# A re-ordered instruction plan and more filler matmuls at the start of a window-attention and gated-FFN kernel

## The chip, the cores and the metric

The kernel runs on one core of one Trainium2 chip. The metric is the device time of one execution, in microseconds (us). The engines are TensorE (PE in the profile, its weight loads PEld), VectorE (DVE), ScalarE (ACT), GpSimd (POOL) and SyncE (SP), whose queue issues every DMA of this kernel.

## The reference

Attention over a causal window of 64 tokens, eight batches of 576 tokens with eight heads of 64, and then a gated feed-forward layer on the 4608 resulting rows:

```python
scores = scale * np.matmul(q, k.transpose(0, 1, 3, 2))
mask = (rel >= 0) & (rel < window)                      # window = 64
scores = np.where(mask, scores, -1000000000.0)
attn = softmax(scores); x = np.matmul(attn, v)          # x: 4608 x 512
h = x @ w_in                                            # 512 x 2048, float64 values
sp = np.maximum(h, 0.0) + np.log1p(np.exp(-np.abs(h)))  # softplus
out = (h * erf(sp)) @ w_out                             # 2048 x 512, float64 values
```

## The kernel before

Every product is made from a high and a low float16 part (three matmuls for one), with power-of-two scales that come from the largest magnitudes of the data. Attention works in 36 units u of 128 tokens. Two units are a chunk c of 256 tokens, and each chunk goes through the feed-forward layer in two halves of the hidden width, so there are 36 groups g.

The weights arrive as float64 and are turned into scaled float16 pairs on the chip, in 16 pieces u of 1 MB (pieces 0 to 7 of `w_in`, 8 to 15 of `w_out`). This conversion runs beside the first units of attention, and the stretch up to about 200 us in which it goes on is called the prologue here.

Nothing is scheduled at run time. `PLAN` is one string of tokens; each token calls one handler, and each engine executes its instructions in the order in which the tokens stand. A number after the name is the unit, piece, group or pair, and a last letter is the engine (a ScalarE, v VectorE, g GpSimd). The tokens that matter below:

- `L` loads a weight piece; `lq lk lv` load q, k and v of a unit; `t` and `xt` are transposing transfers of the attention weights and of x. All of them are on SP's queue.
- Weight conversion: `g` makes a plane of sign bits (one buffer, so one piece at a time), `d` builds the low bits from it, and `dd` does both on VectorE without the plane; `c` rebiases, `o` assembles, `b` takes the largest magnitude. For each pair of pieces `mb` (TensorE), `mx` (VectorE), `my` (TensorE) and `mc` (VectorE) turn that into a scale on all partitions. `dg` (a scaled diagonal) and `h` make the high part, `lp` (TensorE) and `le`, or `l`, the low part.
- Chunk scale: `pk` peaks of q, k and v, then `pa` (VectorE), `pb` (TensorE), `px` (VectorE), `py` (TensorE), `pc` (VectorE).
- Attention: `qh ql kh kl vh vl` the float16 parts, `s` scores, `m` masked maximum, `f e r` softmax, `a` weights times v, `n` normalize, `xh xl` the parts of x.
- Feed-forward: `mm:g:p` the first matmuls (24 for each p of 0 to 3), `ev` their eviction, `sp er gt gh gl` the gate, `mA mB` the second matmuls, `fo st` the result.
- `wm:k:n` is n matmuls of the identity into an unused part of a PSUM tile, which nothing reads. They only keep TensorE occupied.

The PSUM tile `av` holds five things: the output of `a`, the small rows and columns written by `pb`, `py`, `mb` and `my`, and the target of `wm`:

```python
    crow, call = avb[:3, 0, row_at:row_at + P], avb[:, 0, row_at + P:row_at + P + 3]
    wrow, wall = avb[:1, 1, row_at:row_at + P], avb[:, 1, row_at + P:row_at + P + 1]
    idle = avb[:, 0, row_at + P + 3:row_at + P + 123]
    ...
    def warm(k, n):
        for _ in range(n):
            nc.tensor.matmul(idle, ident, ident[:, :120], start=True, stop=True)
```

An instruction that reads `av` waits for TensorE by a count. In the built program this count reaches to the last TensorE instruction that wrote `av` ahead of the reader in `PLAN`, and matmuls of `wm` are among those: where a `wm` token stands between `py` and `pc`, `pc` waits for the end of that `wm`.

Of the kernel before, what the change touches and what calls it, by code (L numbers as in the profile page):

```python
# [19 lines left out]
W = 64  # L20
# [193 lines left out]
def window_attention_gated_ffn(ctx, tc, q, k, v, w_in, w_out, masks, out):  # L214
# [195 lines left out]
    def expo(u, par):  # L410
        s, es = smi(u, par), cde[u // TPC][:, 1:2]
        nc.scalar.activation(pp[0][u % 2][:, HP * par:HP * par + HP, :], s, AF.Exp, bias=shift14, scale=es)  # L412
        nc.scalar.activation(s, s, AF.Exp, bias=shift14, scale=es)  # L413
# [298 lines left out]
```

## Time and profile before

| | us |
|---|---|
| median of 3 runs | 932.47 (932.11 to 933.4) |
| the profiled execution, its own time | 931.69 |
| its span, first to last instruction | 929.5 |
| TensorE busy | 897.9 (97%), of which 32.7 are `wm` (line 643, 507 matmuls) |
| VectorE, ScalarE, GpSimd busy | 714.7, 634.4, 290.8 |
| mean granted TensorE clock | 0.993 |

Time outside the span is 2.2 us (931.69 less 929.5). A row of a timeline gives the start and the length of instructions in us, then engine, line, operation, and output <- input by tile; in brackets is how long the engine was idle just before, and who released it. The line numbers of `wm` are 643 before and 647 after the change, those of the other functions behind `expo` move by four as well.

### The profile page before, as it was taken

To read this page: it belongs to the slowest core of one execution; us is meant where nothing else is said; L and a number is where in the kernel's file an instruction comes from. 1 tells how busy PE (TensorE), PEld (TensorE's weight loads), DVE (VectorE), ACT (ScalarE), POOL (GpSimd) and SP (SyncE) were. 2 spreads that over 40 slices of the span, in tenths; PEclk is the share of its full clock that TensorE was granted. 3 is DMA by queue.
4 is the path that set the end of the run, shared out by engine and by line. 5 is a ranking of instruction groups with operands and counts; after the bars stand their busy time and mean duration, and the time that the engine had idled before them with its cause. 6 is when DMAs were issued, how large, how long until landed. Compare 5 with 4: busy or idle time off the path is not lost.

```text
span 929.5 us, 22240 instructions
## 1 busy us (share of the span) xinstructions
PE 897.9 (97%) x9281; PEld 603.5 (65%) x9281; DVE 714.7 (77%) x1506; ACT 634.4 (68%) x749; POOL 290.8 (31%) x299
## 2 busy tenths in 40 slices
PE   8779998999999999999999999999999999999998
PEld 8546566656766666667666767566667566766663
DVE  6989887988888998785976876986876976845443
ACT  4888976888675886959764758764768764924333
POOL 1343333425244353441330541330541430501000
PEclk9989999999999999999999999999999999999999
DMA  9585747144443555445353525352625250301000
GB/s 366 171 199 182 202 86 197 41 96 132 112 129 81 114 128 124 84 111 102 93 86 102 113 88 103 92 92 102 112 84 103 91 105 33 70 23 24 24 23 23
DMA packets 140532, 98.63 MB, mean 106 GB/s; under 512 B 117776, under 2 KB 117904, under 8 KB 140432
## 3 DMA queue, kind: packets, MB, share of 16 engines
q1 hardware_dynamic: 140432, 97.22, 42.2%
q8 instruction: 72, 1.18, 0.5%
q14 instruction: 28, 0.23, 0.1%
HBM read 59.44 MB, written 9.44 MB: 74 GB/s over the span
## 4 chain that ended last, share of the span: by engine, by line
PE 79%; DVE 10%; DMA 5%; ACT 3%; issue 1%; POOL 1%; DVEq 0%; POOLq 0%; ACTq 0%
PE hp L590 36%; PE o L626 35%; PE av L427 3%; PE s L394 2%; DMA vr<-v_in 2%; PE o L553 1%; DMA stage<-w_out 1%; DVE y L610 1%; DMA qr<-q_in 1%; DVE gl L322 1%; DMA xt<-xs 1%; DMA stage<-w_in 1%; DVE vs L322 1%; DVE sm L403 1%; DVE stage L504 1%
## 5 line engine op out<-in xcount | busy, mean ns | idle before, releaser
L590 PE MATMUL hp<-xt,w 128*128 128x256 f16 x3456 | 401.8, 274 | 7.8 <-DMA xt<-xs 3.6
L590 PEld LDWEIGHTS <-w 128*128 128x128 f16 x3456 | 336.7, 98 | 70.4 <-issue 11.4
L626 PE MATMUL o<-w,gh 128*128 128x512 f16 x1152 | 260.9, 379 | 2.5 <-DVE w L444 1.8
L626 PEld LDWEIGHTS <-gh 128*128 128x128 f16 x1152 | 110.3, 98 | 125.8 <-issue 2.4
L317 DVE TENSOR_SCALAR h<-hp,c 128x512 f32<-128x512 f32 x123 | 90.9, 745 | 79.4 <-PE hp L590 79.0
L626 PE MATMUL o<-w,gl 128*128 128x512 f16 x576 | 136.4, 380 | 0.0
L602 ACT ACTIVATE y<-h 128x1024 f32<-128x1024 f32 x72 | 73.6, 1052 | 91.3 <-DVE h L317 90.1
L408 POOL TENSOR_TENSOR sm<-sm,mx 128x512 f32<-128x512 f32 x66 | 71.7, 1099 | 105.8 <-DVE mx L403 105.5
L322 DVE SCALAR_TENSOR_TENSOR gl<-y,sg,gh 128x1024 f16<-128x1024 f32 x72 | 97.4, 1354 | 5.8 <-PE o L626 4.0
L610 DVE TENSOR_TENSOR y<-h,y 128x1024 f32<-128x1024 f32 x72 | 95.3, 1333 | 8.4 <-ACT y L606 8.2
L626 PEld LDWEIGHTS <-gl 128*128 128x128 f16 x576 | 54.1, 98 | 56.3 <-DVE gl L322 0.5
L450 POOL TENSOR_TENSOR xs<-x,xs 128x512 f16<-128x512 f32 x32 | 46.5, 1453 | 140.3 <-ACT xs L442 107.8
L606 ACT ACTIVATE y<-y 128x1024 f32<-128x1024 f32 x72 | 73.7, 1050 | 0.5
L403 DVE CUSTOM_DVE_ANT_0 sm<-s,mask 128x128 f32<-128x128 f32 x288 | 64.5, 285 | 9.9 <-PE s L394 5.2
L417 POOL TENSOR_TENSOR p<-sm,p 128x512 f16<-128x512 f32 x39 | 53.4, 1371 | 47.2 <-ACT sm L413 46.9
L412 ACT ACTIVATE p<-sm,shift,cde 128x512 f16<-128x512 f32 x72 | 58.1, 807 | 13.0 <-POOL sm L408 12.6
L315 ACT ACTIVATE gh<-y,sg 128x1024 f16<-128x1024 f32 x39 | 44.6, 1143 | 30.3 <-DVE y L610 26.3
L602 ACT ACT_TABLE_LOAD x47 | 60.3, 1283 | 0.8
L413 ACT ACTIVATE sm<-sm,shift,cde 128x512 f32<-128x512 f32 x72 | 58.6, 814 | 2.4
L319 POOL TENSOR_SCALAR vs<-vr,csc 128x1024 f16<-128x1024 f32 x28 | 34.6, 1237 | 78.8 <-PE av L427 67.7
L322 DVE SCALAR_TENSOR_TENSOR vs<-vr,csc,vs 128x1024 f16<-128x1024 f32 x36 | 52.5, 1462 | 6.3 <-POOL vs L319 5.9
L579 POOL TENSOR_SCALAR sg<-rw,csc,isw 128x2 f32<-128x2 f32 x33 | 17.9, 543 | 117.0 <-DVE cde L366 117.0
(140 smaller groups left out, 991.9 us busy)
## 6 DMA issues: line engine op xcount, KB each, us to landing
vr<-v_in SPq DMA_DIRECT2D x36, 512.0 KB, 4.4
kr<-k_in SPq DMA_DIRECT2D x36, 384.0 KB, 3.8
qr<-q_in SPq DMA_DIRECT2D x36, 256.0 KB, 2.8
out<-ob SPq DMA_DIRECT2D x36, 256.0 KB, 2.1
stage<-w_out SPq DMA_DIRECT2D x6, 1024.0 KB, 5.6
stage<-w_in SPq DMA_DIRECT2D x4, 1024.0 KB, 5.2
w<-w_in SPq DMA_DIRECT2D x2, 1024.0 KB, 11.0
w<-w_out SPq DMA_DIRECT2D x2, 1024.0 KB, 6.4
```

Source lines behind the costliest of these rows:

```text
L317: nc.vector.tensor_scalar(dst, src, s, None, op0=ALU.mult)
L322: nc.vector.scalar_tensor_tensor(dst, src, s, hi, op0=ALU.mult, op1=ALU.subtract)
L403: nc.vector.tensor_tensor_reduce(smi(u, par)[:, j, :], sps[par][:, j, :], mask[:, var, :], 1.0, LOWEST, op0=ALU.add, op1=ALU.max, accum_ou ...
L408: eng_of(eng).tensor_tensor(s, s, m.unsqueeze(2).broadcast_to([P, HP, P]), op=ALU.subtract)
L412: nc.scalar.activation(pp[0][u % 2][:, HP * par:HP * par + HP, :], s, AF.Exp, bias=shift14, scale=es)
L413: nc.scalar.activation(s, s, AF.Exp, bias=shift14, scale=es)
L417: eng_of(eng).tensor_tensor(pp[1][u % 2][:, sl, :], smi(u, par), pp[0][u % 2][:, sl, :], op=ALU.subtract)
L590: nc.tensor.matmul(hps[pc % 2][:, f, :], w1[a][:, cc, fs], xt[b][c % 2][:, cc, :], start=(n == 0), stop=(n == 3 * NCC - 1))
L602: nc.scalar.activation(at(yb, g, n), at(hb, g, n), AF.Softplus)
L606: nc.scalar.activation(y, y, AF.Erf)
L610: nc.vector.tensor_tensor(y, at(hb, g, n), y, op=ALU.mult)
L626: nc.tensor.matmul(ops[j], a[:, f, ts], w2[b][:, hf * GF + f, :], start=f == 0 and a is gh and b == 0, stop=f == GF - 1 and a is gl)
```

## The change

The whole string `PLAN` is replaced, 2356 tokens by 2353. Handlers, buffers and arithmetic stay; `expo` gains an engine argument and a new handler `expo_top` is defined, but no token of the new plan calls it, and all `e` tokens run as before. The core of the diff, with the first lines of the table:

```diff
-    "wm:0:183 L:0 L:1 L:2 lq:0 L:3 L:4 lk:0 lm lq:1 lk:1 lv:1 lv:0 L:5 dd:0 c:0:g o:0 dd:1 b:0:a g:2:a c:1:v o:1 "
-    "pk:0:0:a d:2 b:1:a c:2:v mb:0 wm:1:61 dd:3 o:2 g:4:a c:3:v mx:0 o:3 my:0 wm:2:47 b:2:a d:4 pk:0:1:a mc:0 b:3:a "
...
+    "wm:0:200 L:0 L:1 L:2 L:3 lk:0 lq:0 lm L:4 lk:1 lv:0 lv:1 lq:1 L:5 g:0:g d:0 c:0:g dd:1 o:0 c:1:a g:2:a o:1 "
+    "b:0:a d:2 b:1:a g:3:g c:2:a mb:0 wm:1:11 d:3 pk:0:0:a mx:0 c:3:g my:0 wm:2:69 pk:0:1:a mc:0 o:2 dg:0 h:1:a o:3 "
...
-    def expo(u, par):
+    def expo(u, par, eng="a"):
...
-        nc.scalar.activation(pp[0][u % 2][:, HP * par:HP * par + HP, :], s, AF.Exp, bias=shift14, scale=es)
+        if eng == "a":
+            nc.scalar.activation(pp[0][u % 2][:, HP * par:HP * par + HP, :], s, AF.Exp, bias=shift14, scale=es)
...
+    def expo_top(u, par, eng):
+        eng_of(eng).tensor_copy(pp[0][u % 2][:, HP * par:HP * par + HP, :], smi(u, par))
```

The `wm` tokens have these sizes, in order: before 183, 61, 47, 7, 14, 9, 15, 30, 16, 48, 41, 11, 5, 6, 14 (507 in all, the last one ahead of `mA:0:0`); after 200, 11, 69, 79, 15, 54, 8, 57, 9, 6, 15, 39 (562, the last one ahead of `mm:4`). The block of 79 stands between `py:0` and `pc:0`, that of 57 between `a:0:0` and `n:0`, that of 39 between `py:3` and `pc:3`.

Engines change too. Over the whole plan, `kh` and `qh` go mostly from ScalarE to GpSimd (28 and 30 of 36 on GpSimd, before 4 and 2), `gn`, `dc` and `xl` mostly from GpSimd to VectorE (30, 32 and 30 on VectorE, before 3, 3 and 4), `gh` from ScalarE to VectorE (64 of 72, before 33), and `ev` the other way (75 of 144 on ScalarE, before 21).

First place, VectorE, about 18 to 23 us into the run before: `mx:0` is `wtop<-av`, `mc:0` is the `kw1`, `sw1` pair, the L504 (now L508) rows are `o`, `w2_0`, `w2_1` and `h1` are slots that hold weight pieces 2, 3 and 4. Before:

```order
L504 SCALAR_TENSOR_TENSOR w2_0_140<-w2_0_140 128x1024
L498 TENSOR_SCALAR w2_1_141<-w2_1_141 128x1024
L519 TENSOR_REDUCE wtop_81<-av_153 1x1
L504 SCALAR_TENSOR_TENSOR w2_1_141<-w2_1_141 128x1024
L486 SCALAR_TENSOR_TENSOR h1_143<-h1_143,plane0_84 128x1024
L307 TENSOR_SCALAR kw1_65<-av_153 128x1
L310 TENSOR_SCALAR sw1_66<-kw1_65 128x1
```

And after:

```order
L490 SCALAR_TENSOR_TENSOR w2_1_141<-w2_1_141,plane0_84 128x1024
L523 TENSOR_REDUCE wtop_81<-av_153 1x1
L307 TENSOR_SCALAR kw1_65<-av_153 128x1
L310 TENSOR_SCALAR sw1_66<-kw1_65 128x1
L508 SCALAR_TENSOR_TENSOR w2_0_140<-w2_0_140 128x1024
L508 SCALAR_TENSOR_TENSOR w2_1_141<-w2_1_141 128x1024
```

The two conversion instructions that stood between `mx:0` and `mc:0` are gone from there: `o:2` and `o:3` now stand behind `mc:0`, and `d:4` has become a `dd:4` behind them.

Second place, VectorE around `pc:0` (the rows `cpw` to `cde`), the scale that the float16 parts of units 0 and 1 need. Before:

```order
L357 TENSOR_REDUCE ctop_79<-av_153 3x1
L358 SCALAR_TENSOR_TENSOR cdiag_80<-ctop_79,ident_82 3x3
L561 TENSOR_REDUCE wm1_67<-kw1_65 128x1
L310 TENSOR_SCALAR isw_68<-wm1_67 128x1
L364 COPY cpw_76<-av_153 128x3
L310 TENSOR_SCALAR csc_77<-cpw_76 128x3
L366 TENSOR_SCALAR cde_78<-cpw_76 128x1
```

And after:

```order
L358 SCALAR_TENSOR_TENSOR cdiag_80<-ctop_79,ident_82 3x3
L364 COPY cpw_76<-av_153 128x3
L310 TENSOR_SCALAR csc_77<-cpw_76 128x3
L366 TENSOR_SCALAR cde_78<-cpw_76 128x1
L367 TENSOR_SCALAR cde_78<-cpw_76 128x1
L494 TENSOR_SCALAR y1_145<-y1_145 128x1024
L495 SCALAR_TENSOR_TENSOR y1_145<-y1_145 128x1024
```

`W:0` is no longer between `px:0` and `pc:0`, `pc:0` follows `px:0` directly, and `dd:5` (the two `y1` rows) stands behind it.

Third place, VectorE around `n:0` (`den0` to `x0`). Before:

```order
L322 SCALAR_TENSOR_TENSOR vs1_0_116<-vr0_104,csc_77,vs0_0_114 128x16x64
L504 SCALAR_TENSOR_TENSOR stage0_149<-stage0_149 128x1024
L432 TENSOR_SCALAR den0_96<-av_153 128x8
L433 RECIPROCAL rd0_98<-den0_96 128x8
L434 TENSOR_TENSOR x0_129<-av_153,rd0_98 128x2x4x64
```

And after:

```order
L322 SCALAR_TENSOR_TENSOR vs1_0_116<-vr0_104,csc_77,vs0_0_114 128x16x64
L508 SCALAR_TENSOR_TENSOR stage1_150<-stage1_150 128x1024
L436 TENSOR_SCALAR den0_96<-av_153 128x8
L437 RECIPROCAL rd0_98<-den0_96 128x8
L438 TENSOR_TENSOR x0_129<-av_153,rd0_98 128x2x4x64
```

Here VectorE's row of instructions hardly moves; what stands on TensorE between the last `a:0` matmul and `n:0` goes from 11 filler matmuls to 57.

More of the change, by code (lines that the diff above doesn't have):

```diff
@@ L650, in window_attention_gated_ffn @@
         "qh": q_hi, "ql": q_lo, "kh": k_hi, "kl": k_lo, "vh": v_hi, "vl": v_lo, "s": scores, "m": masked_max,
-        "f": shift, "e": expo, "r": expo_rest, "t": turn, "a": weigh, "n": normalize, "xh": x_hi, "xl": x_lo,
+        "f": shift, "e": expo, "y": expo_top, "r": expo_rest, "t": turn, "a": weigh, "n": normalize, "xh": x_hi, "xl": x_lo,
         "xt": x_turn, "L": fetch, "g": sign_plane, "d": low_bits, "dd": low_bits2, "c": rebias, "o": assemble,
```

320 rows, old and new, of the table PLAN are left out of this document.

## The prediction

> **What bounds the kernel now.** I read the page's busy shares and slices first, then busy time by stage, then TensorE's timeline through the prologue, and last what VectorE waited for there.
>
> ```profile
> span 929.5 us, 22240 instructions
> PE 897.9 (97%) x9281; PEld 603.5 (65%) x9281; DVE 714.7 (77%) x1506; ACT 634.4 (68%) x749; POOL 290.8 (31%) x299
> PE   8779998999999999999999999999999999999998
> 0.00:34.00 34.00, 27.76 (x403) 23.59 (x403) 25.20 (x43) 20.10 (x30) 5.21 (x20) 1.00 0.77 293
> 34.00:69.20 35.20, 26.88 (x345) 16.45 (x334) 30.31 (x78) 28.03 (x41) 18.14 (x13) 0.90 0.80 202
> 69.20:109.90 40.70, 37.13 (x439) 26.93 (x438) 34.51 (x90) 36.18 (x53) 17.89 (x18) 1.00 0.64 178
> 109.90:158.10 48.20, 41.77 (x494) 29.09 (x494) 43.27 (x101) 37.86 (x48) 14.23 (x12) 0.96 0.64 152
> 158.10:266.00 107.90, 105.79 (x1063) 68.43 (x1063) 92.92 (x205) 83.94 (x99) 44.73 (x43) 0.98 0.40 101
> 266.00:930.00 664.00, 658.61 (x6555) 439.00 (x6552) 488.45 (x995) 428.31 (x481) 190.61 (x196) 1.00 0.37 84
> ```
>
> The last six rows are stretches: start:end, length, then busy time of PE, PEld, DVE, ACT and POOL, granted clock, DMA share and GB/s. From 158 us on TensorE is busy all but 7.5 us of 771.9 (107.90 less 105.79, and 664.00 less 658.61, in which the empty 0.5 us past the span's end is counted). Its useful work is the same in both plans, token for token. So the end of the run is the time TensorE spends without useful work, plus a constant, and that time lies before 158 us. There TensorE's busy share flatters, since filler counts as busy:
>
> ```profile
> 19.96 2.68 PE L643 MATMUL av<-ident 128*128 128x120 bf16 x47
> 28.90 0.16 PE L361 MATMUL av<-cdiag,ones 3*128 3x3 bf16 x1
> 28.99 0.65 PE L643 MATMUL av<-ident 128*128 128x120 bf16 x9
> 33.39 0.75 PE L394 MATMUL s<-ks,qs 64*64 64x128 f16 x40 [0.41 <-DVE qs L322]
> 69.19 5.40 PE L590 MATMUL hp<-xt,w 128*128 128x256 f16 x48
> 109.95 3.61 PE L626 MATMUL o<-w,gh 128*128 128x512 f16 x16 [1.82 <-DVE w L444]
> 129.52 9.69 PE L590 MATMUL hp<-xt,w 128*128 128x256 f16 x72 [2.01 <-ACT h L315]
> 158.09 12.11 PE L590 MATMUL hp<-xt,w 128*128 128x256 f16 x95 [3.56 <-DMA xt<-xs]
> 171.29 5.41 PE L590 MATMUL hp<-xt,w 128*128 128x256 f16 x48
> ```
>
> The first large block of useful work, `mm:0`, begins at 69.19 us. TensorE has the same useful tokens ahead of it in both plans (scores, `a`, `lp`), so when it begins is one half of the question; how TensorE runs from there to 158 us is the other. Up to 69.2 VectorE is the busiest (25.20 + 30.31 = 55.5 us), ScalarE has 48.1 and GpSimd 23.4. VectorE is therefore what the start hangs on, and its idle time is what to look at:
>
> ```profile
> 22.68 0.16 DVE L307 TENSOR_SCALAR kw<-av 128x1 int32<-128x1 int32 x1 [0.60 <-PE av L643]
> 29.68 0.16 DVE L364 COPY cpw<-av 128x3 f32<-128x3 f32 x1 [0.58 <-PE av L643]
> 61.75 0.17 DVE L432 TENSOR_SCALAR den<-av 128x8 f32<-128x8 f32 x1 [0.65 <-PE av L643]
> ```
>
> These three are released by filler. `mc:0` starts at 22.68, 0.04 us after the end of the 47 fillers (19.96 + 2.68 = 22.64), though nothing of them is read by it; `pc:0` starts at 29.68, 0.04 us after the nine (29.64), though `py:0` was done at 29.06. So a filler block that stands ahead of a reader of `av` is waited for whole. One filler takes 2.68 / 47 = 57 ns.
>
> **The change, part by part.** VectorE's work ahead of `mm:0`, by comparing the tokens of both plans up to there (the forms that differ, and one of the plane on GpSimd):
>
> ```profile
> L498 DVE TENSOR_SCALAR w<-w 128x1024 f32<-128x1024 f32 x2 | 1.4, 688 | 0.0
> L512 DVE TENSOR_REDUCE acc<-h 128x1 f32<-128x1024 f32 x1 | 1.2, 1204 | 0.0
> L317 DVE TENSOR_SCALAR w<-stage,sw 128x1024 f16<-128x1024 f32 x3 | 2.2, 750 | 0.0
> L408 DVE TENSOR_TENSOR sm<-sm,mx 128x512 f32<-128x512 f32 x6 | 4.1, 679 | 0.0
> L444 DVE CAST xs<-x 128x512 f16<-128x512 f32 x5 | 2.1, 415 | 0.0
> L343 DVE TENSOR_REDUCE peaks<-kr 128x1 f32<-128x768 f32 x28 | 25.6, 946 | 0.2 <-DMA kr<-k_in 0.2
> L480 POOL TENSOR_SCALAR plane<-w 128x1024 f16<-128x1024 f32 x1 | 1.3, 1338 | 0.0
> L480 POOL TENSOR_SCALAR plane<-stage 128x1024 f16<-128x1024 f32 x1 | 2.3, 2279 | 5.7 <-DVE qs L322 5.7
> L504 DVE SCALAR_TENSOR_TENSOR w<-w 128x1024 int32<-128x1024 int32 x4 | 4.9, 1216 | 0.0
> 51.86 0.96 PE L427 MATMUL av<-vs,pt 128*64 128x65 f16 x47 [1.19 <-DVE vs L322]
> ```
>
> Term 1, work leaves VectorE: four `c` (4 x 0.69), one `b` (1.20), `h:1` (0.75), one `f` (0.68), `xh:0` (0.42), and one more k peak comes (0.95). Sum -4.9 us. ScalarE takes three of the `c` and the `b` and gives up two planes, GpSimd takes the rest; both had 21 us or more of idle time before 69.2, which is their cover. If VectorE did not set the start, the term would be 0; as it is the busiest by 7 us I take it whole.
>
> Term 2, waits for filler. `mc:0` follows `mx:0` directly on VectorE now, with 69 fillers (69 x 57 ns = 3.9 us) begun only after `my:0`: it waits all of them, 3.3 more than the 0.60 before. The two `o` that hid most of the 47 before now stand behind it. ScalarE stops there too, since `dg:0` needs that scale and `h:1`, `b:2`, `b:3`, `c:4` queue behind it. `pc:0` follows `px:0` directly, with 79 fillers behind `py:0`: 4.5 us, 3.9 more than the 0.58 before. Behind it stand `dd:5`, `kl:0`, `ql:1`, `ql:0`, and the scores wait for those. `n:0`: the 0.96 us of `a:0` and 57 fillers (3.2) run against one `o` of 1.2 us: 3.0, where before none was left over. `mc:2` behind 54 fillers has 3.2 us of VectorE work beside them and loses about 0.6; `n:1` and `mc:3` come out even (0.65 less, 0.5 more). Sum +10.7. Bounds: 0, if VectorE were late for another reason each time, to +12.3 (69, 79, 57 and the 11 ahead of `mx:0`, all unhidden, 216 x 57 ns). The rows at 22.68 and 29.68 show the wait to the last filler, so I take the upper part.
>
> Term 3, the sign planes. Piece 0 now goes over the plane on GpSimd ahead of `d:0`; that replaces the wait for `c:0:g`, about even. `d:3` must wait for a plane on GpSimd that can begin only when `d:2` has freed the one buffer: 1.34 us, at worst 2.28. +1.4.
>
> Together `mm:0` begins 7.2 us later, at 76.4. Adding the rows' durations along the queues, from the first load's landing on, gives the same picture at the stations: `mc:0` begins at 21.3 (before 22.68), `pc:0` at 35.0 (before 29.68), the scores of unit 0 at 40.6 (before the main part at 33.39; `pc` 0.5, `dd:5` 1.9, `kl` 1.0, `qh` 0.5 and two `ql` 1.5 lie between), `n:1` at 70 (before 61.75).
>
> Term 4, from `mm:0` to `mm:4`. Three waits of TensorE in before are quoted above, 1.82 + 2.01 + 3.56 = 7.4 us. Two of them were followed by slow matmuls: 72 took 9.69 and 95 took 12.11, where 48 at full clock took 5.41, so 1.6 and 1.4 us too much. What becomes of them:
>
> ```profile
> 150.00 0.58 SPq L474 DMA_DIRECT2D stage<-w_out  x1
> 151.19 1.20 SPq L454 DMA_TRANSPOSE xt<-xs  x1
> 151.19 6.86 DMA xt<-xs
> xt<-xs SPq DMA_TRANSPOSE x72, 2.7
> ```
>
> The transfer of x for `mm:4` took 6.86 us, against a median of 2.7, issued 1.2 us after a 1 MB load. In the new plan both `xt:5` still stand behind `L:15` on SP's queue, and 39 fillers (2.2 us) stand where TensorE would wait. The wait stays, the slow clock after it should go: -1.4. But `pc:3` waits for those 39 with the rest of VectorE's queue behind it; half of 2.2 is taken, +1.1. The 2.01 us hung on `ev:2` behind the softmax of units 4 and 5, whose q load `lq:6` now stands earlier in SP's queue: half of 2.01 + 1.6, -1.8. Ahead of `mA:0` the 14 fillers go, -0.8, and the eviction moves to ScalarE. Fifteen fillers come ahead of `a:5`, +0.9. Sum -2.0, between -10.4 (all waits and slow matmuls go) and +3.1 (none goes, and 39 and 15 fillers come on top).
>
> The Trainium skill, TensorE: Matmul & The Clock Gate, section on why this matters for your kernels, wants no idle gap of TensorE over about 3 us, since the clock then falls to half. Here a gap of 2.01 us was already followed by slow matmuls, and one of 1.82 us was not, so the measured limit decides. By the page's limit only the 3.56 gap would cost clock, and Term 4 would be -1.2 in place of -2.0. The page also speaks against this change: the gap between the 79 fillers and the scores comes out at 5.6 us, over either limit.
>
> Term 5, the steady part. TensorE has no slack to give there and can only lose.
>
> ```profile
> L319 POOL TENSOR_SCALAR qs<-qr,csc 128x512 f16<-128x512 f32 x2 | 3.6, 1814 | 8.3 <-PE av L361 6.2 <-PE av L427 2.0
> L319 POOL TENSOR_SCALAR ks<-kr,csc 128x768 f16<-128x768 f32 x4 | 4.5, 1143 | 6.1 <-issue 6.1
> L315 ACT ACTIVATE qs<-qr,csc 128x512 f16<-128x512 f32 x30 | 20.1, 710 | 32.1 <-DVE csc L310 32.1
> L322 DVE SCALAR_TENSOR_TENSOR ks<-kr,csc,ks 128x768 f16<-128x768 f32 x36 | 36.6, 1049 | 0.0
> ```
>
> `qh` on GpSimd takes 1.81 (two samples) for ScalarE's 0.71. Between `py` and the scores lie two `qh` and a `kh` on GpSimd and a `kl` on VectorE, 3.6 + 1.1 + 1.05, and with the short `pc` about 6.5 us; TensorE has two `mm` and one `mB` to do meanwhile, 2.7 each (half of 5.41) and 1.8 (half of 3.61), 7.2 us. It just fits: 0, up to +0.7 in each of 14 chunks if GpSimd runs slower.
>
> Sum: -4.9 + 10.7 + 1.4 - 2.0 = +5.2. The profiled execution took 931.69 (span 929.5 and 2.2 around it), so 936.9 against it. It lies 0.8 below the median of 932.47, which makes 937.7.
>
> **The rivals.** A, the forecast: VectorE waits out the filler and the start moves back by about 7 us.
>
> B, faster: the waits of TensorE after 69 us go, because the plan now expects the transfers late. Place: `mA:0`, `mm:2`, `mm:4`. Price -10.4, which with the +7.2 of the start gives 932.47 - 3.2 = 929.3, and with a start only 3 us late 925.1. It decides once more than 7.2 us of the 10.4 go (9.1 for a gain that can be measured). For it: these are three waits on named late work, and slow matmuls follow two of them. Against it: the third wait is still planned (39 fillers), and VectorE works 43.27 of 48.20 us there, so an earlier TensorE soon meets it.
>
> C, the two cancel: of the 10.4 some 5.3 to 9.1 go, which leaves -1.9 to +1.9, within 0.2%, about what a measurement of this kernel can tell from no change.
>
> D, slower still: GpSimd's `qh` and `kh` make TensorE wait before the scores in each chunk, 14 x 0.7 = 9.8 more, 947.5.
>
> **How the numbers follow.** A has 0.64, B 0.13, C 0.12, D 0.11. A and D are slower, 0.75. A alone reaches from 934.5 (Term 4 at -5) to 943 (Term 4 at +3.1). The range takes in C and the near part of B and D: 930 to 946.
>
> **What would show it.** In the changed profile `kw` begins some 4 us after `my:0` and `cpw` about 4.5 us after `py:0`, both released by the fillers of L647; TensorE idles some 5 us between the 79 fillers and the scores; the 24-matmul blocks of `mm:0` begin near 76 us; the matmuls of `mm:4` follow their fillers at full clock. I am wrong if `mm:0` begins before 70 us, if `cpw` starts right after `py:0`, or if TensorE after 270 us loses more than it did (5.4 us of 664).

## The result, and the profile after

The changed kernel takes 944.63 us (median of 6 runs, 943.07 to 946.78), the kernel before 932.93 beside it (6 runs, 930.74 to 938.62). The ratio is 1.0117 with a 95% interval of 1.0084 to 1.0149 (the two medians alone give 1.0125): 1.2% slower. The forecast was 937.7, so the direction came out as argued and the size 6.9 us too small. The profiled execution took 943.07, its span is 941.2.

The page of the changed kernel, and its first and last stretch (columns as in the prediction: length, busy PE, PEld, DVE, ACT, POOL, granted clock, DMA share, GB/s):

```profile
span 941.2 us, 22432 instructions
PE 902.2 (96%) x9336; PEld 606.6 (64%) x9336; DVE 720.7 (77%) x1561; ACT 635.6 (68%) x784; POOL 288.3 (31%) x247
0.00:82.01 82.01, 58.77 (x750) 41.84 (x751) 53.73 (x113) 48.73 (x71) 32.03 (x39) 0.88 0.69 208
270.00:942.00 672.00, 665.58 (x6631) 442.48 (x6629) 499.27 (x1079) 433.31 (x527) 186.67 (x151) 1.00 0.37 86
```

The span is 11.7 longer: TensorE is busy 4.3 more, all of it filler and slower matmuls, and idle 7.4 more. `mm:0` begins at 82.01 in place of 69.19, 12.8 later, and from there to the end pass 859.2 us in place of 860.3, 1.1 less. The whole loss lies ahead of `mm:0`. TensorE's timeline there, and around `mm:4`:

```profile
18.31 3.85 PE L647 MATMUL av<-ident 128*128 128x120 bf16 x69
31.93 0.16 PE L361 MATMUL av<-cdiag,ones 3*128 3x3 bf16 x1 [0.87 <-DVE cdiag L358]
32.02 4.39 PE L647 MATMUL av<-ident 128*128 128x120 bf16 x79
41.34 0.43 PE L394 MATMUL s<-ks,qs 64*64 64x128 f16 x8 [4.92 <-DVE qs L317]
61.96 3.21 PE L647 MATMUL av<-ident 128*128 128x120 bf16 x57
82.01 5.40 PE L594 MATMUL hp<-xt,w 128*128 128x256 f16 x48
164.81 2.25 PE L647 MATMUL av<-ident 128*128 128x120 bf16 x39
168.35 5.40 PE L594 MATMUL hp<-xt,w 128*128 128x256 f16 x48 [1.29 <-DVE h L317]
```

Now VectorE of the changed kernel, its longest idle times ahead of `mm:0` and all that filler releases:

```profile
7.46 1.23 DVE L490 SCALAR_TENSOR_TENSOR stage<-stage,plane 128x1024 int32<-128x1024 int32 x1 [7.46 <-POOL plane L484]
16.75 1.23 DVE L490 SCALAR_TENSOR_TENSOR w<-w,plane 128x1024 int32<-128x1024 int32 x1 [1.48 <-POOL plane L484]
22.20 0.16 DVE L307 TENSOR_SCALAR kw<-av 128x1 int32<-128x1 int32 x1 [4.04 <-PE av L647]
36.45 0.16 DVE L364 COPY cpw<-av 128x3 f32<-128x3 f32 x1 [4.57 <-PE av L647]
54.57 0.16 DVE L307 TENSOR_SCALAR kw<-av 128x1 int32<-128x1 int32 x1 [1.58 <-PE av L647]
65.21 0.17 DVE L436 TENSOR_SCALAR den<-av 128x8 f32<-128x8 f32 x1 [3.06 <-PE av L647]
72.52 0.16 DVE L307 TENSOR_SCALAR kw<-av 128x1 int32<-128x1 int32 x1 [0.69 <-PE av L647]
78.87 0.69 DVE L448 CAST w<-o 128x512 f16<-128x512 f32 x1 [2.46 <-PE o L558]
```

`mc:0` (22.20) starts 0.04 us after the last of the 69 fillers (18.31 + 3.85), `pc:0` (36.45) 0.04 after the last of the 79, `n:0` (65.21) 0.04 after the last of the 57. The 79 fillers end at 36.41 and the scores begin at 41.34: TensorE was kept busy up to the moment at which VectorE could start, and then waited 4.92 us for VectorE. The same view of the kernel before, the waits that the prediction did not show:

```profile
5.99 0.70 DVE L490 TENSOR_SCALAR stage<-stage 128x1024 int32<-128x1024 int32 x1 [5.99 <-DMA stage<-w_in]
9.20 1.23 DVE L504 SCALAR_TENSOR_TENSOR stage<-stage 128x1024 int32<-128x1024 int32 x1 [1.25 <-POOL stage L496]
38.12 0.69 DVE L343 TENSOR_REDUCE peaks<-qr 128x1 f32<-128x512 f32 x1 [1.30 <-DMA qr<-q_in]
49.68 0.69 DVE L343 TENSOR_REDUCE peaks<-vr 128x1 f32<-128x512 f32 x1 [1.60 <-DMA vr<-v_in]
66.05 0.69 DVE L444 CAST w<-o 128x512 f16<-128x512 f32 x1 [0.93 <-PE o L554]
```

That gives the account of the 12.8 us. VectorE is busy 53.7 up to `mm:0` where it was 55.5, -1.8, and idle 82.0 - 53.7 = 28.3 where it was 13.7, +14.6:

| VectorE idle ahead of `mm:0`, us | before | after | difference |
|---|---|---|---|
| released by filler (`kw`, `cpw`, `den`) | 1.83 | 13.94 | +12.1 |
| the first load, sign planes, the first `c` | 7.24 | 8.94 | +1.7 |
| q and v loads | 2.90 | 0 | -2.9 |
| `le:5:0` (`w<-o`), which waits for `lp:5` | 0.93 | 2.46 | +1.5 |
| other waits, each under 1 us | 0.8 | 3.0 | +2.2 |

The +1.5 at `le:5:0` is not the clock: `lp:5` runs at the lower clock in both kernels (two matmuls in 2.02 us before, in 2.08 after). In the new plan `n:1` stands ahead of `pb:1`, and `lp:5` behind it, so TensorE waits 1.81 us for `n:1` (at 74.29) before `lp:5` can begin.

### The profile page after: what moved, and what is told of

Its sections match the earlier page's. It is cut to its first block, busy times and chain, and to the rows that moved or that the text cites. A ratio compares the mean times of both kernels' runs of the same rounds, so it can differ in the third digit from the quotient of the medians.

```text
span 941.2 us, 22432 instructions
## 1 busy us (share of the span) xinstructions
PE 902.2 (96%) x9336; PEld 606.6 (64%) x9336; DVE 720.7 (77%) x1561; ACT 635.6 (68%) x784; POOL 288.3 (31%) x247
## 4 chain that ended last, share of the span: by engine, by line
PE 75%; DVE 12%; ACT 7%; issue 2%; DMA 2%; POOL 1%; DVEq 0%; POOLq 0%; ACTq 0%
PE o L630 34%; PE hp L594 32%; PE av L431 3%; PE s L394 2%; PE av L647 2%; PE o L557 2%; DVE vs L322 1%; DVE y L614 1%; DMA pt<-p 1%; ACT L606 1%; DVE stage L495 1%; ACT y L606 1%; DMA stage<-w_out 1%; DVE stage L508 1%; DVE qs L322 1%
## 5 line engine op out<-in xcount | busy, mean ns | idle before, releaser
L315 ACT ACTIVATE h<-hp,c 128x512 f32<-128x512 f32 x75 | 48.3, 679 | 148.4 <-PE hp L594 148.3
L408 POOL TENSOR_TENSOR sm<-sm,mx 128x512 f32<-128x512 f32 x66 | 81.7, 1252 | 156.9 <-DVE mx L403 152.4
L322 DVE SCALAR_TENSOR_TENSOR gl<-y,sg,gh 128x1024 f16<-128x1024 f32 x72 | 101.5, 1418 | 11.6 <-PE o L630 10.6
L614 DVE TENSOR_TENSOR y<-h,y 128x1024 f32<-128x1024 f32 x72 | 88.2, 1243 | 17.3 <-ACT y L610 16.9
L319 POOL TENSOR_SCALAR qs<-qr,csc 128x512 f16<-128x512 f32 x30 | 23.0, 777 | 204.2 <-issue 150.4
L421 POOL TENSOR_TENSOR p<-sm,p 128x512 f16<-128x512 f32 x40 | 57.2, 1431 | 85.0 <-ACT sm L414 67.3
L317 DVE TENSOR_SCALAR h<-hp,c 128x512 f32<-128x512 f32 x69 | 51.2, 745 | 36.6 <-PE hp L594 36.5
L403 DVE CUSTOM_DVE_ANT_0 sm<-s,mask 128x128 f32<-128x128 f32 x288 | 64.2, 284 | 14.8 <-PE s L394 14.6
L317 DVE TENSOR_SCALAR gh<-y,sg 128x1024 f16<-128x1024 f32 x64 | 54.3, 857 | 15.8 <-PE o L630 15.4
L322 DVE SCALAR_TENSOR_TENSOR vs<-vr,csc,vs 128x1024 f16<-128x1024 f32 x36 | 50.3, 1397 | 9.2 <-POOL vs L319 9.1
L319 POOL TENSOR_SCALAR vs<-vr,csc 128x1024 f16<-128x1024 f32 x29 | 49.8, 1717 | 20.3 <-PE av L431 18.7
```

Source lines behind the costliest of these rows:

```text
L317: nc.vector.tensor_scalar(dst, src, s, None, op0=ALU.mult)
L319: nc.gpsimd.tensor_scalar(dst, src, s, 1.0, op0=ALU.mult, op1=ALU.mult)
L322: nc.vector.scalar_tensor_tensor(dst, src, s, hi, op0=ALU.mult, op1=ALU.subtract)
L403: nc.vector.tensor_tensor_reduce(smi(u, par)[:, j, :], sps[par][:, j, :], mask[:, var, :], 1.0, LOWEST, op0=ALU.add, op1=ALU.max, accum_ou ...
L408: eng_of(eng).tensor_tensor(s, s, m.unsqueeze(2).broadcast_to([P, HP, P]), op=ALU.subtract)
L614: nc.vector.tensor_tensor(y, at(hb, g, n), y, op=ALU.mult)
```

## The experiments

Theory F: a reader of `av` waits out the whole filler block ahead of it, VectorE's queue waits with it, and this is the loss. Ratios are to the kernel before on the same chip, with a 95% interval; "behind" is the time from the start of `mm:0` to the end of the span. Tokens in the diffs are pieces of `PLAN`. `mm:0` and "behind" are read from one profiled execution of each kernel, and executions of one kernel differ by some us (e9: 927.43 to 933.8), so a difference of 1 or 2 us in these two columns is not shown by them alone.

| kernel | `mm:0` at | behind | ratio |
|---|---|---|---|
| before | 69.19 | 860.3 | 1 |
| changed | 82.01 | 859.2 | 1.0117 [1.0084, 1.0149] |
| e1_fill_behind | 72.18 | 857.2 | 1.0001 [0.9981, 1.0020] |
| e2_no_three | 73.17 | 857.1 | 1.0015 [0.9999, 1.0030] |
| e3_before_big | 79.54 | 862.7 | 1.0122 [1.0080, 1.0165] |
| e4_no_late | 83.98 | 857.4 | 1.0122 [1.0089, 1.0156] |
| e5_behind_pc | 80.79 | 858.2 | 1.0097 [1.0080, 1.0114] |
| e6_behind_mc | 80.79 | 862.2 | 1.0140 [1.0125, 1.0155] |
| e7_before_behind | 70.30 | 858.8 | 1.0015 [1.0001, 1.0029] |
| e8_off_gpsimd | 70.81 | 857.7 | 0.9993 [0.9980, 1.0007] |
| e9_all_mended | 69.31 | 857.1 | 0.9988 [0.9968, 1.0008] |
| e10_before_no_fill | 67.64 | 854.8 | 0.9957 [0.9935, 0.9980] |
| e11_mended_no_fill | 70.20 | 857.4 | 0.9981 [0.9969, 0.9994] |
| e12_after_no_fill | 70.94 | 856.2 | 0.9985 [0.9967, 1.0002] |

**e1_fill_behind, the changed plan with the same filler behind the readers.**

```diff
-my:0 wm:2:69 pk:0:1:a mc:0
+my:0 pk:0:1:a mc:0 wm:2:69
-py:0 wm:3:79 dg:1 pc:0
+py:0 dg:1 pc:0 wm:3:79
-a:0:0 wm:7:57 le:4:0:a t:1:0 n:0
+a:0:0 le:4:0:a t:1:0 n:0 wm:7:57
 (likewise wm:5:54 behind mc:2, wm:8:9 behind mc:3, wm:11:39 behind pc:3)
```

> The changed kernel with the same fillers, but the blocks of 69, 79, 54, 57, 9 and 39 stand behind mc:0, pc:0, mc:2, n:0, mc:3 and pc:3 in the plan and no longer ahead of them, so these readers wait only for the matmul they read. Theory F (readers wait out the filler): kw starts within 0.5 us of my:0 and cpw within 0.5 us of py:0, the scores of unit 0 come 7 to 8 us earlier than 42.7, mm:0 near 72 in place of 82, and the time is 8 to 11 us under that of the changed kernel, about 934 to 937. Theory Q (the order of the conversion itself, with its sign planes on GpSimd, sets the start): mm:0 no earlier than 79, at most 3 us gained.

The time falls back to that of before, ratio 1.0001. VectorE and TensorE of this kernel (its line numbers are six higher than those of the changed one):

```profile
18.32 0.16 DVE L313 TENSOR_SCALAR kw<-av 128x1 int32<-128x1 int32 x1 [0.25 <-PE av L532]
28.43 0.16 DVE L370 COPY cpw<-av 128x3 f32<-128x3 f32 x1 [0.25 <-PE av L367]
28.65 7.13 PE L653 MATMUL av<-ident 128*128 128x120 bf16 x79 [0.25 <-DVE cpw L370]
35.71 0.86 PE L400 MATMUL s<-ks,qs 64*64 64x128 f16 x48
```

The two readers are released by the matmul that they read, within 0.25 us. The 79 fillers now take 7.13 us, since the clock was down, and cost little: the scores follow them at once, and VectorE begins on the scores at 36.62, where it does so at 36.05 in e2, without these fillers. The mere place of matmuls that nothing reads (268 of the 307 moved stand ahead of `mm:0`) is worth 9.8 us of start.

**e2_no_three, the changed plan without the blocks of 69, 79 and 57.**

```diff
-my:0 wm:2:69 pk:0:1:a mc:0
+my:0 pk:0:1:a mc:0
 (likewise without wm:3:79 and wm:7:57)
```

> The changed kernel without the blocks of 69, 79 and 57. F: the same gain as with the blocks behind their readers, 934 to 937; if the filler kept the clock up for useful work, this one is 1 to 3 us slower than that. Q: at most 3 us gained on the changed kernel.

`mm:0` at 73.17, ratio 1.0015. Leaving the three out gives nearly what moving them gives: `mm:0` is 1.0 later than in e1, and the intervals of the two ratios overlap. The mean clock is 0.983, in e1 0.990, so a small worth of the filler for the clock, as put ahead, is possible and not shown.

**e3_before_big, the same waits put into the plan before.**

```diff
-wm:2:47
+wm:2:69
-py:0 wm:5:9 L:6 pc:0
+py:0 wm:5:79 L:6 pc:0
-wm:11:11 dg:2 n:0
+wm:11:57 dg:2 n:0
```

> The kernel before, with three of its blocks brought to the sizes of the changed one at the same places: 47 to 69 (ahead of mc:0), 9 to 79 (ahead of pc:0), 11 to 57 (ahead of n:0). F: mc:0 waits 1.2 us more, pc:0 4.0, n:0 up to 2.6, so 6 to 8 us slower than before. Q: TensorE had idle time there, within 2 us of before.

Three numbers of the old plan make it as slow as the new one: 1.0122, `mm:0` 10.3 later, VectorE's waits 1.77 (`kw`), 4.32 (`cpw`) and 3.63 (`den`), all released by filler. That is more than the 6 to 8 us of F: the three waits alone account for 8.5 us more than before, and `mx:0` waits 1.18 for the 61 fillers, which took 4.88 us in place of 3.43. With e1 and e2 the theory holds from both sides, in its mechanism if not in the size, and order and engines of the other tokens are not needed for the loss.

**e4_no_late, the changed plan without the 15 fillers ahead of `a:5` and the 39 ahead of `mm:4`.**

```diff
-wm:10:15
-wm:11:39
```

> The changed kernel without its last two blocks (15 ahead of a:5, 39 between py:3 and pc:3). F: pc:3 no longer waits 2.2 us, but TensorE then idles 3.5 to 4 us ahead of mm:4 and its next matmuls run at a lower clock: between 2 us faster and 2 us slower than the changed kernel. If the late blocks were what the gain after mm:0 rests on, 2 us or more slower.

Behind `mm:0` pass 857.4 in place of 859.2, so these two blocks may cost some 1.8 us there. That is not shown: the changed kernel, e5 and e6 have the same plan behind `mm:0` and differ by up to 4.0 us there, and the ratio (1.0122) has no gain. In the profiled run `mm:0` itself came 2 us later: its 69 fillers took 5.47 us at the lower clock, where 3.85 in the changed kernel's, and `kw` waited 5.66.

**e5_behind_pc and e6_behind_mc, one block at a time.**

```diff
-py:0 wm:3:79 dg:1 pc:0
+py:0 dg:1 pc:0 wm:3:79
```

> The changed plan with one token moved: the 79 fillers stand behind pc:0 instead of ahead of it. Theory F (a reader of av waits out the whole block ahead of it): cpw begins 0.25 us after py:0 in place of 4.57, mm:0 at about 77.7 us in place of 82.0, time about 4.3 us below the changed kernel, 1.007 to 1.008 times before. Rival H (the block only covers another late wait): cpw begins early, but the scores or mm:0 still come within 1 us of where they were, ratio 1.011 to 1.013.

```diff
-my:0 wm:2:69 pk:0:1:a mc:0
+my:0 pk:0:1:a mc:0 wm:2:69
```

> The changed plan with one token moved: the 69 fillers stand behind mc:0 instead of ahead of it. Theory F: kw of mc:0 begins 0.25 us after my:0 in place of 3.75 to 4.04, mm:0 at about 78.4 us, ratio 1.007 to 1.009. Rival H (VectorE and ScalarE have slack up to pc:0, which later waits take up): mm:0 within 1 us of 82.0, ratio 1.011 to 1.013.

Each wait goes, and yet neither number of F comes: `mm:0` at 80.79 in both, only 1.2 earlier, ratios 1.0097 and 1.0140. TensorE and VectorE of e5_behind_pc show why:

```profile
18.40 5.48 PE L653 MATMUL av<-ident 128*128 128x120 bf16 x69
23.92 0.16 DVE L313 TENSOR_SCALAR kw<-av 128x1 int32<-128x1 int32 x1 [5.66 <-PE av L653]
33.87 0.16 DVE L370 COPY cpw<-av 128x3 f32<-128x3 f32 x1 [0.25 <-PE av L367]
62.35 0.17 DVE L442 TENSOR_SCALAR den<-av 128x8 f32<-128x8 f32 x1 [4.06 <-PE av L653]
75.92 0.69 DVE L454 CAST w<-o 128x512 f16<-128x512 f32 x1 [2.75 <-PE o L564]
76.76 2.05 PE L563 MATMUL o<-stage,diag 128*128 128x512 f32 x2 [0.76 <-DVE cpw L370]
```

The `cpw` wait is gone, but the 69 fillers ahead of it took 5.48 in this run, where 3.85, so `cpw` begins only 2.6 earlier (33.87 against 36.45). The next block takes its part too: `n:0` comes early enough to wait 4.06 for the 57 fillers, where it waited 3.06. At `le:5:0` (75.92 against 78.87) 3.0 us of gain are left. Then the last `lp` runs at the lower clock, 2.05 for what took 1.14 in the changed kernel, and 1.7 more go. The prices of blocks do not add up: with one gone, the next is waited for longer, and the clock after the gap decides about 2 us. In e6 the 3.0 us at `le:5:0` shrink likewise, and 3.0 more are lost behind `mm:0`: up to the 39 fillers it takes 85.8 us at a clock of 0.96, the changed kernel 82.8 at 0.98. There a gap of 1.80 us (at 103.43) was followed by 24 matmuls in 4.45, where 2.78 is full clock. H, as put for e5 and e6, is nearer for the start; the waits themselves are F's.

**e7_before_behind, the plan before with its own blocks moved.**

```diff
-mb:0 wm:1:61
+wm:1:61 mb:0
-my:0 wm:2:47 b:2:a d:4 pk:0:1:a mc:0
+my:0 b:2:a d:4 pk:0:1:a mc:0 wm:2:47
 (likewise 14, 9, 41, 11, 5, 14 behind mc:1, pc:0, mc:2, n:0, n:1, n:3, and 7 ahead of mb:1)
```

> The kernel before, with its own blocks of filler placed so that none stands between a TensorE result in av and its reader (47, 14, 9, 41, 11, 5 and the 14 ahead of n:3 behind mc:0, mc:1, pc:0, mc:2, n:0, n:1, n:3; 61 and 7 ahead of mb:0 and mb:1). Theory F: the 0.60, 0.58 and 0.65 us before kw, cpw and den go to about 0.25, and the 2.1 us den wait goes: 1.0 to 3.5 us less, ratio 0.996 to 0.999. Rival J (in the plan before, the blocks are hidden by other VectorE work and something else is late next): ratio 0.999 to 1.001, mm:0 within 0.5 us of 69.2.

No gain: 1.0015 and `mm:0` 1.1 later, nearest to J and a little worse than its ranges. TensorE and VectorE of this kernel:

```profile
22.32 4.36 PE L648 MATMUL av<-ident 128*128 128x120 bf16 x54 [2.18 <-DVE kw L312]
26.61 0.33 PE L521 MATMUL av<-ident,acc 128*1 128x128 bf16 x3
26.98 0.28 DVE L524 TENSOR_REDUCE wtop<-av 1x1 bf16<-1x128 f32 x1 [2.66 <-PE av L521]
```

The 47 and 7 fillers (one block of 54 now) no longer stand ahead of `mc:0`, but `mb:1` stands behind them, and VectorE waits 2.66 us for that in place of 0.60. So filler behind a reader is harmless only where the next matmul that somebody waits for comes late enough.

**e8_off_gpsimd, the suspected cause of the small VectorE gain.** On top of e1:

```diff
-h:0:g
+h:0:a
-g:6:g
+g:6:a
```

> The changed plan with its fillers behind their readers (as in e1_fill_behind), and two conversion steps, h:0 and the sign plane g:6, on ScalarE in place of GpSimd. Theory G (the work moved to GpSimd slows VectorE's instructions beside it, which is why VectorE gained little from it): the tensor_scalar of dd:4 takes 0.70 us in place of 1.63, the one of qh:0 0.48 in place of 1.58, VectorE's busy time up to mm:0 falls by 2 us from 54.5, and mm:0 begins at 70 to 71 us in place of 72.2, ratio 0.997 to 0.999. Rival K (ScalarE becomes late by its 2.6 us of added work): VectorE's durations fall, but mm:0 stays at 72 to 74 us, ratio 1.000 to 1.002.

GpSimd and VectorE beside each other in e1, and VectorE alone in e8:

```profile
18.83 3.23 POOL L325 TENSOR_SCALAR w<-stage,sw 128x1024 f16<-128x1024 f32 x1
31.42 1.57 POOL L490 TENSOR_SCALAR plane<-stage 128x1024 f16<-128x1024 f32 x1 [3.25 <-DMA stage<-w_in]
20.99 1.63 DVE L500 TENSOR_SCALAR h<-h 128x1024 int32<-128x1024 int32 x1
31.68 1.58 DVE L323 TENSOR_SCALAR qs<-qr,csc 128x512 f16<-128x512 f32 x1
```

```profile
21.09 0.68 DVE L500 TENSOR_SCALAR h<-h 128x1024 int32<-128x1024 int32 x1
32.77 0.48 DVE L323 TENSOR_SCALAR qs<-qr,csc 128x512 f16<-128x512 f32 x1
0.00:70.80 70.80, 55.66 (x750) 41.51 (x751) 52.60 (x113) 50.82 (x73) 31.73 (x37) 0.93 0.77 241
```

With GpSimd quiet, the same two instructions take 0.68 and 0.48 in place of 1.63 and 1.58. In e1 both began while a GpSimd row was running and ended 0.56 and 0.27 us after its end, as if they had waited for it. VectorE's busy time up to `mm:0` falls from 54.5 to 52.6, and `mm:0` comes 1.4 earlier (G's 70 to 71). The ratio, 0.9993, lies between the ranges of G and K, and its interval reaches into both: of the start G is shown, of the time neither. The Trainium skill, GPSIMD Engine Reference, section Key points, says that GpSimd shares its SBUF interfaces with VectorE and contends with some VectorE instructions; it gives no size, and the trace agrees with a factor of 2.4 to 3.3.

**e9_all_mended, every late step ahead of `mm:0` moved.** On top of e8:

```diff
-g:0:g d:0
+dd:0
-g:3:g
-d:3
+dd:3
-r:1:0:g c:7:a lp:4:1 vl:0 e:1:1:a
+r:1:0:g e:1:1:a c:7:a lp:4:1 vl:0
 (and mb:3 behind a:1:1, dg:3 ahead of h:6:a, wm:7:57 as wm:7:40)
```

> The kernel of e8_off_gpsimd with the late steps ahead of mm:0 that its trace shows moved: dd:0 and dd:3 in place of the sign planes on GpSimd (VectorE waited 1.47 us for the second), e:1:1 ahead of c:7 on ScalarE (its exponentials release the transfer that a:1 waits for), mb:3 behind a:1, dg:3 ahead of h:6 (lp:5 waited for it), and 40 fillers in place of 57 ahead of a:1. If VectorE's chain sets the start, as theories F and G say: mm:0 at 66.5 to 68.5 us in place of 70.8, ratio 0.995 to 0.998. Rival L (what is won ahead of mm:0 is given back behind it, since the loads and transfers of the next units keep their times): mm:0 early, but the stretch from mm:0 to the end grows from the 857.1 to 859 us of the runs so far to 860 or more, ratio 0.998 to 1.001.

`mm:0` at 69.31, 1.5 earlier than in e8 and not the 66.5 to 68.5 expected; ratio 0.9988, no difference that is shown. L fails, as 857.1 pass behind it. One edit aimed at a wait that was not there: TensorE's row shows what it waited for before `lp:5`, not `dg:3` but `n:1`, since `pb:1` stands ahead of `lp:5` and writes the `av` that `n:1` reads. It is the wait that makes the +1.5 at `le:5:0` in the changed kernel.

```profile
61.86 0.22 PE L359 MATMUL av<-ident,cmx 128*3 128x128 bf16 x1 [1.29 <-DVE x L444]
```

**e10_before_no_fill, the kernel before without its 324 fillers after the first 183.**

```diff
-wm:1:61 wm:2:47 wm:3:7 wm:4:14 wm:5:9 wm:6:15 wm:7:30
-wm:8:16 wm:9:48 wm:10:41 wm:11:11 wm:12:5 wm:13:6 wm:14:14
```

> The kernel before without any filler but the first 183 (324 matmuls fewer). Theory M (filler holds up the clock, and that is worth more than the waits it makes): the granted clock between 20 and 80 us falls to 0.6 to 0.8, lp and a run at half speed, mm:0 1 to 4 us later than 69.2, ratio 1.002 to 1.008. Rival N (filler of the prologue buys nothing there): no reader of av waits for it, mm:0 at 67 to 69 us, ratio 0.995 to 1.001.

The fastest kernel of the study by its median: 926.99 us against 931.26, ratio 0.9957 [0.9935, 0.9980]. Two stretches of the kernel before, and then the same two of this one with three rows of its TensorE:

```profile
20.00:65.00 45.00, 34.55 (x480) 22.83 (x480) 39.68 (x98) 38.34 (x57) 17.64 (x12) 0.93 0.77 215
65.00:170.00 105.00, 94.23 (x1035) 67.08 (x1033) 88.27 (x209) 82.92 (x115) 35.55 (x36) 0.96 0.58 150
```

```profile
20.00:65.00 45.00, 28.67 (x239) 11.59 (x238) 40.63 (x101) 38.44 (x58) 16.96 (x13) 0.65 0.77 217
65.00:170.00 105.00, 96.64 (x1116) 70.02 (x1117) 96.14 (x230) 90.33 (x124) 41.53 (x37) 1.00 0.56 155
46.28 2.07 PE L557 MATMUL o<-w,diag 128*128 128x512 f32 x2 [3.28 <-DVE w L448]
67.64 5.40 PE L594 MATMUL hp<-xt,w 128*128 128x256 f16 x48
151.60 10.53 PE L594 MATMUL hp<-xt,w 128*128 128x256 f16 x95 [1.85 <-DMA xt<-xs]
```

M had the clock right, 0.65 in place of 0.93 from 20 to 65 us, and the time wrong: TensorE has slack there (28.67 of 45 us busy), VectorE has little (40.63). The Trainium skill, TensorE: Matmul & The Clock Gate, section on why this matters for your kernels, wants no idle gap over about 3 us; the row at 46.28 agrees as to the clock (a gap of 3.28, then 2.07 us for two matmuls that take 1.17 at full clock), and the shorter time of the whole shows that following its advice did not pay here, where VectorE sets the pace. N had the start, 67 to 69. From 65 us on the clock is 1.00 where it was 0.96, and the wait ahead of `mm:4` is 1.85 us with full-speed matmuls after it, where it was 3.56 with matmuls at the lower clock. Of the 5.5 us by which the stretch behind is shorter, 20 fillers fewer are some 1.4, the shorter wait ahead of `mm:4` 1.7 and the full clock after it 1.6; the rest was not separated. The profiled execution was also the fastest of the ten (924.65, median 926.99), so the profiles show more gain than the ratio, 7.0 us against some 4.

**e12_after_no_fill and e11_mended_no_fill complete the table of orders with and without filler.** Each is its plan (the changed one, and that of e9) with every `wm` but `wm:0:200` left out:

```diff
-wm:1:11 wm:2:69 wm:3:79 wm:4:15 wm:5:54 wm:6:8 wm:7:57 wm:8:9 wm:9:6 wm:10:15 wm:11:39
```

> The changed plan without any filler but the first 200. It completes the table of two orders, each with and without filler (the kernel before without filler had ratio 0.9957). Theory F (the loss of the changed kernel is its filler, and its order alone brings nothing): mm:0 at 69 to 71 us, ratio 0.994 to 0.999. Rival O (the order itself is worse, through the work on GpSimd and the short distance from px:0 to pc:0): mm:0 at 72 to 75 us, ratio 0.999 to 1.005.

`mm:0` at 70.94 in place of 82.01, ratio 0.9985: theory F. From 1.0117 to 0.9985 are 1.3%, some 12 us: the filler of the changed kernel costs this much. In the kernel before it costs 0.4%.

> The kernel of e9_all_mended without any filler but the first 200. If filler in the prologue costs more than the clock it holds (as the kernel before without filler showed: mm:0 at 67.64 us in place of 69.19, and 854.8 us from there to the end in place of 860.3), mm:0 at 67 to 69 us, 853 to 856 us behind it, ratio 0.990 to 0.995. Rival P (this order has already no reader that waits for filler, so that only the slower clock is new): mm:0 at 70 to 72 us, ratio 0.998 to 1.003.

`mm:0` at 70.20, as rival P said, 857.4 behind, ratio 0.9981, at the lower edge of its range. Where no reader waits for filler, taking it out makes the start 0.9 us later (69.31 in e9), which bounds what the held clock is worth here; the ratios of the two (0.9981 and 0.9988) show no difference. The three orders without filler have ratios of 0.9957, 0.9985 and 0.9981 with intervals that overlap, so which of them is best is not shown.

## Why the prediction was right, and where its sizes were off

**The mechanism held.** `kw` some 4 us after `my:0` and `cpw` about 4.5 after `py:0` (VectorE waited 4.04 and 4.57 us for them), TensorE idle some 5 us before the scores (4.92), `mm:4` at full clock after its fillers (48 in 5.40): these signs came as named. The start of `mm:0` near 76 did not: it was 82.01. Of the three signs of being wrong, two did not come; the third came by its letter, but small: the lost time of TensorE after 270 us is 672.00 - 665.58 less the 0.8 past the span's end, 5.6 us in 671, against 4.9 in 664 before.

**The range held with little to spare.** 944.63 lies in 930 to 946, but above the 943 up to which rival A alone was to reach. The room above 943 was given for D, which did not come, so that the time is inside the range is in part luck.

**The sum** was +5.2 and came out at +11.7. By its terms:

| term | forecast | measured |
|---|---|---|
| 1, work leaves VectorE | -4.9 | -1.8 |
| 2, waits for filler | +10.7 | +12.1 |
| 3, sign planes | +1.4 | +1.7 |
| not in the sum: q and v loads, `le:5:0`, small waits | 0 | +0.8 |
| 4, `mm:0` to `mm:4` | -2.0 | -1.1, with the steady part |

**Term 1 is the step that failed**: 3.1 of the 6.5 us. The instructions did leave VectorE, and their rows add up to the 4.9 us forecast. But the rows that stayed add up to 2.2 more, 1.8 of it in the three `TENSOR_SCALAR` rows of `dd`; and rows that overlap their neighbours, which busy time counts once, overlap by 6.1 us in place of 7.0, another 0.9. Two of the `dd` rows now run beside GpSimd: `h:0`, which came there from ScalarE, and `c:0`, which was on GpSimd before too, only that VectorE waited for it then (1.25 us, at 9.20). VectorE and GpSimd of the changed kernel, and after them the same GpSimd step of the kernel before, when VectorE stood idle:

```profile
8.61 1.61 DVE L494 TENSOR_SCALAR stage<-stage 128x1024 int32<-128x1024 int32 x1
24.73 1.58 DVE L494 TENSOR_SCALAR h<-h 128x1024 int32<-128x1024 int32 x1
37.44 0.68 DVE L494 TENSOR_SCALAR y<-y 128x1024 int32<-128x1024 int32 x1
7.51 2.16 POOL L500 TENSOR_SCALAR stage<-stage 128x1024 f32<-128x1024 f32 x1
22.64 3.12 POOL L319 TENSOR_SCALAR w<-stage,sw 128x1024 f16<-128x1024 f32 x1 [3.68 <-DVE sw L310]
37.49 1.39 POOL L319 TENSOR_SCALAR ks<-kr,csc 128x768 f16<-128x768 f32 x1
```

```profile
8.04 1.12 POOL L496 TENSOR_SCALAR stage<-stage 128x1024 f32<-128x1024 f32 x1 [4.56 <-DVE stage L491]
```

The first two VectorE rows began while the first two GpSimd rows were running, end 0.55 us after them, and cost 1.8 us over the third; e8 shows the same for two rows by moving the GpSimd work. The third VectorE row had GpSimd beside it too, but began 0.05 us ahead of it: it kept 0.68, and GpSimd's row took 1.39, where the same step took 0.90 in the kernel before. So not every overlap costs VectorE; in these rows the instruction that began second is the longer one.

**Term 2** was right block by block (`mc:0` +3.4 for +3.3, `pc:0` +4.0 for +3.9, `n:0` +3.1 for +3.0), except `mc:2`, forecast at 0.6 because 3.2 us of VectorE work would hide the 54 fillers, and measured at 1.58: only 1.5 us of that work lay beside them (51.48 to 52.99). The bounds, 0 to 12.3, held it barely, and left the blocks of 54 and 9 out, whose waits (1.58 and 0.69) are in the 12.1. In e4, e5 and e6 the 69 fillers take 5.46 to 5.48 us, 79 ns for one in place of 57, which no bound had in it.

**Term 4** went both ways as put: the matmuls at the lower clock at `mm:4` are gone, and the wait of 2.01 us is down to 0.78 (at 138.92) with full clock after it. But 24 matmuls just ahead of `mm:4` (at 157.97) took 3.92 us, where 2.78 is full clock, and `pc:3` waits 2.80 us for the 39 fillers, where half of 2.2 was taken. What the two late blocks cost together is not shown (e4).

**The rivals.** B fails: with the start undone (e1) the stretch behind gains 3.1 us on before, not 10.4. D fails: 0.7 us more idle time of TensorE in the steady part, not 9.8.

## What to carry to other kernels

Filler that writes a buffer which others read acts, in a build like this one, as a lock on that buffer: where an order by hand or a planner puts it between a result and its reader, the reader's engine waits for every one of its matmuls. Before adding filler to hold the clock, ask from the profile whether TensorE is late in that stretch at all; here VectorE was, and a run without filler, the cheapest experiment of this study, had the lowest median. When work is moved to a free engine, price the instructions that will run beside it anew.

## What was not expected of the hardware

- A 128x1024 VectorE tensor_scalar of 0.68 us takes 1.58 to 1.63 when it begins while a GpSimd tensor_scalar is running, and GpSimd's own goes from 1.12 to 2.16: both lose, so work moved to GpSimd can cost VectorE time. In the one row shown where VectorE's began first, it kept 0.68 and GpSimd's alone was longer (1.39 for 0.90).
- A granted clock of 0.65 in place of 0.93 through 45 us of the prologue (20 to 65 us) made the start 0.9 us later in one profiled execution each (e11 against e9), and cost less than the filler that prevents it (e10). The order of before has the lower clock later with filler than without: 0.96 against 1.00 from 65 to 170 us.
- The block of 69 fillers took 3.84 to 3.85 us in five profiled executions (the changed kernel, e1, e3, e8, e9) and 5.46 to 5.48 in three others (e4, e5, e6), though the changed kernel, e4 and e5 have the same plan up to there: filler cannot be priced to better than that.
- No sharp limit for the gap that lowers the clock shows: gaps of 1.82 (before) and 1.85 us (e10) were followed by matmuls at full clock, one of 1.80 (e6) by matmuls at the lower one. The 2.01 that the prediction used as a limit is one case.
